# GateLoop attention and a PReLU MLP in one program: other banks for the last pair's products, and another written-out order

## The chip, the cores and the metric

The program runs on one core of a Trainium2 chip. The metric is the device time in microseconds (us) of one execution of the whole program; 787.76 us is the median of three runs before the change (786.93 to 790.6). The profile is of one further execution.

## The reference

Two stages. The first is a recurrence over 768 tokens, for 4 batches and 8 heads, with a state of 48 x 48 complex numbers per head; the second is a two-layer MLP on its output, with 384 model columns and 2048 hidden columns.

```python
mag = np.sqrt(a_re * a_re + a_im * a_im)
scale = np.minimum(mag, 0.999) / (mag + 1e-06)
a_re_n, a_im_n = (a_re * scale, a_im * scale)
...
for t in range(S):
    ar, ai = (a_re_n[:, :, t, :, None], a_im_n[:, :, t, :, None])
    new_re = ar * S_re - ai * S_im
    new_im = ar * S_im + ai * S_re
    kv = np.einsum('bhd,bhe->bhde', k[:, :, t], v[:, :, t])
    S_re, S_im = (new_re + kv, new_im)
    y[:, :, t] = np.einsum('bhd,bhde->bhe', q[:, :, t], S_re)
...
h = x @ w_in
g = np.maximum(h, 0.0) + alpha * np.minimum(h, 0.0)
return (g @ w_out).astype(np.float32)
```

The tokens of the first stage, 4 x 768 = 3072 rows of 384, are the rows `x` of the second.

## The kernel before

**Units.** The 3072 tokens are cut into 24 units of 128 tokens (six per batch). `gates` turns the inputs `a_re` and `a_im` of one or several units into phases (`phs`) and running products of decays (`decs`), on VectorE (DVE) and ScalarE (ACT), and writes them to DRAM. `loads` and `loads_v` bring `KQ` (keys and queries), `PP` (phases), `T` (decays), `V` and `VL` (values) of a unit back in. `unit` does the recurrence without a loop over tokens: for six distances (1, 2, 4, 8, 16, 32) it multiplies keys and queries by decays on DVE (L642, six times a unit), copies half of them on ACT (L665, L681), and multiplies keys by queries on TensorE (PE) into the tile `ps_lv` (L601). Then it turns the keys (L713), makes the new states from keys and values (L725, `ps_kv`; L733 and L736 on DVE), multiplies the queries by the states (L751) and the masked key-query products by the values (L765), both into `ps_y`, copies the result to the tile `T` (L778, ACT) and sends it to DRAM (L783). `loads_x` reads two units of it as `xT`, the input of the MLP for a pair of units, 256 rows.

**Weights.** The weights come as 64-bit words and are turned into 32-bit floats in sixteen pieces, by `to_f32`: three ACT steps (L439 to L443) and three DVE steps (L447, L449, L451) for each piece.

**MLP.** There are twelve pairs. `features` (L824, the first two pairs) and `two_features` (L846, the other ten) make hidden columns: products into the tile `ps_h`, which has two buffers of one PSUM bank each, then ACT (L831; L855, L859) and DVE (L833; L861). `outputs` (L874) does the second layer of the first two pairs. For the other ten `seven` does it with seven block products in place of eight (a Strassen-Winograd scheme) in half-size blocks: `product` (L960) puts 8 matmuls of 128 x 192 into the tile `ps_o`, which has one buffer, the ring that the planner calls `sums`; after each product ACT (L976) or DVE (L966, L987, L1003) adds the block to `top0` or `top1`, and L1009 and L1017 send the results to DRAM. The products of one pair are called P1, P2, T2, T1, T3, T4 and P3, in this order. Between the first two the DVE makes sums of blocks of hidden columns (L974, L982, L984, L990); T2 reads what L984 has made. A matmul of 32-bit floats stands in the trace as two matmul rows, a transpose (L713) as one: a product is 16 rows.

**Order.** All of these are Python generators. Each `yield` is a step, with a cost, the steps that it waits for and the rings that it takes a buffer of; these arguments are read by a planner that is not part of the kernel. In the kernel `step` gives `None`, `Ring.put` does nothing, and `Plan.run` takes the next step of the task that the next letter of the string `ORDER` names: A to I are the nine calls of `gates`, J `loads`, K `half_rows`, L `loads_v`, M `pieces` (raw weights), N and O `weights`, P to Z and a to m the 24 units, n `loads_x`, o `all_mlp`. The order in which letters come is the order of instructions on each engine's queue and on the queue of SP, which issues all transfers. What an instruction waits for on the chip follows from the tiles that it reads and writes. Within `all_mlp` the steps have a fixed order of their own, which `blocks`, `some` and `part` set.

```python
def step(*args, **kwargs):
    return None
DVE = ACT = POOL = PE = DMA = step
...
def run(self, order):
    for c in order:
        next(self.tasks[self.LETTERS.index(c)], None)
```

Of the kernel before, what the change touches and what calls it, by code (L numbers as in the profile page):

```python
# [31 lines left out]
    "ABMMAAAABKABBAAAAAAAAAABAAMAAAMMBNABMJKNNBAAABANNBAAAJAANABBBBBAAAAAABAAABBBBBBBJMJJAPPPMOOOOPBJJBBB"  # L32
    "BNBLBOBBBNOONNOBBBPLJJLJJJOOBBBBOBOBLMLCPPPPNNPNNPPCNPPPQPPQOPONCNPCOONOPCCJJLKKKKMLLLLLOQCCQPPPPPPP"
    "PQLLLLJJMJMJMQPPPPPQCQCQCCPQCPCPCPCPPCPPCOQCCPPQQOPPPPPPLCQCNNNCQQCLLJLJJnLJLMJLQNCOOLLJLLLLLLJMCCCC"
    "RRNOQoQCCRQCRQQQRoQQooNCCCoQoQOQooQQoNNRQCRCCQRCQCORNNoQRQQoooooOOOOQRooQQRQRQooQQooQCJQQLLLQRNORRND"
    "DLLJJSoooooooNOONORODORRORSnLLMLLLLJLLLLRDDooooRRooooooDRRoRRRSSNDooooooDoDooRooRooooMoSooSRRDDSJJJM"
    "KDoDRDoRSSSDRDDoooRoDoOooRRRRRORRSoooDDRDDoOJoooooSSLLLLLLoRDoooooDoSSoooooORRMDSoSooooSSoTDJLLLLLJJ"
    "LJLLLJKKKDDKDJSDSSoToDDDSSSTSSoooDDNDSNDNoSSoooTTSTTOSSDTODSoNToooooooNNNDOSSSSSooSSoSSSSDTTJKLNoNoo"
    "ooNoTTToTooooTLSLSDLLnLLLLLoNNTNoooNNooTTTTOTToTToJLLLLoooOoOLJToooTTOOoJEooTToUUoooooooTJJTTUUoEoTT"
    "oJJooTTUTTTUTUEoToTTUoUUooooooTLLLLLLTToVoUEoUoUUooEoUoUooooooUVLLLJVLLEUUUooUUULJJLLooJKJKJJooEUEVo"  # L40
    "oUUoooooUUVooEUUoooVoUVVUVUVVVEoooEVUUUUUUVVUoUUVEULUoVVooooooEULLLLLJJLLLJLLLJLVoEEooVooVoVVoVoooWV"
    "VVEEVVoooooooEoVoLLEoWoooooooooVEWooEoEooWoVoWWVoVEEVVVWWooooooEEJnVVVVVVLWWVoooVWVVoWVVLJWKJJLLLEJW"
    "WWWLLLLJLLELLLLEoJooooooWWooooEooWEWEEEEEoEooooXXEEXEoooWooWWWWJoooooooooooJEJooWWooWoWoooXFWWWWWXXW"
    "WXXWoooXXoooooooooooXWWWWWWWooooooooooooooooXXooooLWWLKnFJLFXXoFXFYYooooooooLLJLLLLLLLLLLJJXoooooooo"
    "oooooXXXYFXXXFooooooXXooXoooooXXoooYFFFXXooooooYYXXYXFYFYooooooYXXYoooooooooooXXXYXXXYYoXXFXXYYYoooo"
    "oooooooFoooooooYYoLLJXLJoFoooooXYFYYFFLLLJLJJLJLoYYYYooZoooooooooooZoooYooLooYoLLLLLoJJFZFooZooooooo"
    "oooooYYZZYoYZYZZZYYZFFFKJJaYooooooooooYYZFFZYYYYYYYKKLLYFFLYLLLLooooJLLnJZZoFoFooooooooFZoaZoooooooo"
    "oFooLFFFJLLLLJoooooFoooZZZZooooZFZooooaFFFFFLFoooZoooooooooooZZoooooZooooZaooooooooooJJJGZoaZaZaZZaa"
    "aoZoZoooooZZZaaoZZZaooooooooZZZZLLZZLLLLLLGGGaaaaooooooooGGooaaooaaaaoaoaaGooooooooooGGGooaooaGooaao"
    "oooooooooooobLLLLJLLaabbabJboooooooobaJJKJJJaaaabaooaaaabobbbooooooooobGbGaacLoooooobboocbooobbooooo"  # L50
    "oLJLJLLLLJLLLLJnbGcGGLJooooooooooocGooGJLLLoooobcGoooobcbbooooooobooooocGbbbbobbooobbooobbcboccGGocG"
    "bbGJdbbbbbbLoooooooooooooooGLGLLLGbbGoocoGbcooobcGcooGoooooooLbLbLooGooooocGcooooooooooooooccccccccG"
    "GodGoococoocoooooocooocoJJLLLJLLLLJJJoocddddGoocGcGoGcoooooocccccccccoJedddccododoGLccHLLLJJoooooooo"
    "oJLLLHLLLooooodddddHdeoooooHHoooooooooonLLLLLoJJoooooddoHeHHKKKdddooddoooooooooodooHoooooooooddoodod"
    "odoooeededHHdedeooHHoeeoddHoodooooooddddeeddddLdJJdLooooooooooeoeHoooeeeooooooooooooHfHooeeoefLLLLJJ"
    "LJLLLLLLLLJJJeeHeooeooooooooooeoooHHeooeoooeooHofHoooooooooooeoooefffeHefefffeeHeooHHfooooooKJHeeeef"
    "eeeoooooooeHeLLLeLLLeHLLLJJoooooooooofgffofHJLnLLLoooooooofHHoLLoHHHoooooooooHooooooffofHHoooooooogo"
    "oofffffoHHHofffoooooooogoogooooofoofooooooogfgfgffgggffoooooHJJJJohgooofffffffffgIIIhoooooooooLLffLh"
    "JJLLLLJJLLLLJJLLLooogoooggooogIgoooooooooooooooooohhhoooooogghhoooIgggIggggoIoogoooogooogogIoooooogg"
    "hhghhgooooooJooooghggghhgggggggoohhIooooIIIooooooooionhIIhJJLLLLJJLLJJLLLLoLLLLoLooooooooooooooooooI"  # L60
    "IoiooooooooiooooooooohhhhhhoIoIiiohooooooooooooooooooohohihhoioooooohhoohhihiihhhhihoIIIoIoohihhihho"
    "oooJhhiiioILLhjoooooooooooooooohooIIjiLJJLLLLLLLIIJLLIoILLLJoojooooooooiioooooooooiiIIjIiooiIIIIIIIi"
    "iioojooooioooooooooiooiiojiJJoijIioojijIijjoooooooiiiiiijiiiiiiJLnoojjjjjokJJoooooooooooLLJJLLLLLLLL"
# [36 lines left out]
def kernel(  # L100
# [422 lines left out]
    def loads_v():  # L523
        for u in range(NU):
            b, c = divmod(u, NCH)
            yield DMA(172, ("KQ", u), takes=(R["V"],))
            L = loaded[u]
            L["V"] = V = work.tile([P, HP, D2], F32, tag="V", name="V", bufs=1)
            nc.sync.dma_start(V[0:P - 16], v[b, :, 1:P - 15, c].rearrange("n p e -> p n e"))
            yield DMA(24)  # L530
            nc.sync.dma_start(V[P - 16:P - 1], v[b, :, P - 15:P, c].rearrange("n p e -> p n e"))
            if c + 1 < NCH:
                yield DMA(2)
                nc.sync.dma_start(V[P - 1:P], v[b, :, 0:1, c + 1].rearrange("n p e -> p n e"))
# [24 lines left out]
            L["Vp"] = {name: VL[:, i] for i, name in enumerate(LEVELS)}  # L559
            done["V", u] = t  # L560
# [7 lines left out]
    def unit(u):  # L568
# [149 lines left out]
        e = yield PE(0.72, e, ("V", u), *[("state", u - 1)] * (u > 0), takes=(R["misc"],) if last else (R["misc"], R["lv"]), mode=2, n=16 if last else 32)  # L718
# [223 lines left out]
    def seven(m, made):  # L942
# [20 lines left out]
        def fold(to, z, e, base, *deps, last=True):  # L963
# [3 lines left out]
            if last:  # L967
                R["sums"].put(t)
# [30 lines left out]
        yield 0  # L999
        z, e = yield from product(apart, T3, "T3", s3)  # L1000
# [4 lines left out]
        yield 0  # L1005
        z, e = yield from product(A22, T4, "T4", s4)
# [4 lines left out]
        yield 0  # L1011
        z, e = yield from product(A12, B22, "P3", s4)
# [127 lines left out]
```

## Time and profile before

| | |
|---|---|
| median of the runs | 787.76 us |
| profiled execution | 792.45 us |
| its span, first to last instruction | 790.7 us |
| what lies around the span | 1.75 us |
| instructions | 26869 |
| moved by DMA | 130.62 MB |
| granted TensorE clock, mean over the span | 0.974 |

In the views below a row of the timeline is: start, duration (both us), engine, line, operation, tiles out<-in, partitions x elements, xcount, and in brackets the engine's idle time before it and what ended it. PEld is the loading of a matmul's weights, which overlaps with PE. SPq is the queue of SP. A window row is: its length, then busy us (and instructions) of PE, PEld, DVE, ACT and POOL, the granted clock, the mean busy share of the 16 DMA engines, and GB/s. The chain of waits lists start, length and what the end of the program was waiting for at that time. Matmul ends are modelled, so lengths of matmuls are best read from start to start.

### The profile page before, as it was taken

What the parts mean: (1) busy time and instruction counts of PE and PEld (TensorE: products, weight loads), DVE (VectorE), ACT (ScalarE), POOL (GpSimd) and SP (SyncE); (2) the same over time, 40 slices, a digit from 0 to 9 for tenths busy, and PEclk for the clock granted to TensorE, in tenths of its full rate; (3) what the DMA queues carried; (4) which work ended last, traced back from release to release, by engine and by line L of the source; (5) the groups of instructions that cost most, each with busy time, mean ns of one, the idle gap of its engine ahead of it and who ended that gap; (6) DMA issues with size and microseconds to landing.
All of it is one profiled execution on the core that took longest, in us unless ns stands there. A gap on an engine that the chain in (4) does not pass through costs nothing.

```text
span 790.7 us, 26869 instructions
## 1 busy us (share of the span) xinstructions
PE 679.4 (86%) x11728; PEld 582.6 (74%) x11728; DVE 613.5 (78%) x815; ACT 493.0 (62%) x933; POOL 12.0 (2%) x48
## 2 busy tenths in 40 slices
PE   0024567698899999999999999999999999999997
PEld 0013445576676788988888888888988888989986
DVE  7899879787988899888897899786897766832331
ACT  8966978774467576777487666846768535443230
POOL 5000000000000000000000000000000000000000
PEclk9998589799999999999999999999999999999999
DMA  8998899869836865586656855683636644421000
GB/s 245 269 311 210 217 280 237 232 195 218 180 102 176 236 173 119 164 246 167 171 145 170 226 159 154 188 222 95 167 99 203 169 105 103 121 43 51 1 21 20
DMA packets 177181, 130.62 MB, mean 165 GB/s; under 512 B 66280, under 2 KB 168424, under 8 KB 176616
## 3 DMA queue, kind: packets, MB, share of 16 engines
q1 hardware_dynamic: 177064, 128.91, 61.4%
q8 instruction: 92, 1.51, 0.9%
q14 instruction: 25, 0.20, 0.1%
HBM read 100.52 MB, written 35.42 MB: 172 GB/s over the span
## 4 chain that ended last, share of the span: by engine, by line
PE 61%; DVE 11%; ACT 10%; DMA 9%; issue 4%; SPq 3%; DVEq 0%; ACTq 0%
PE ps_h L846 20%; PE ps_o L960 19%; PE ps_lv L601 4%; PE ps_o L874 4%; PE ps_h L824 4%; PE ps_y L765 4%; DVE KQ L642 4%; PE ps_kv L725 3%; DMA gate<-in_a_re_dram 2%; PE ps_y L751 2%; DMA T<-decs 2%; PE ps_kt L713 2%; DMA PP<-phs 1%; DMA decs<-gate 1%; DMA shared<-in_w_out_dram 1%
## 5 line engine op out<-in xcount | busy, mean ns | idle before, releaser
L846 PE MATMUL ps_h<-xT,w_in_sb 128*128 128x256 f32 x960 | 228.4, 383 | 1.4 <-DVE shared L861 1.1
L846 PEld LDWEIGHTS ps_h<-xT,w_in_sb 128*128 128x128 f32 x960 | 176.8, 190 | 23.3 <-DVE shared L861 1.5
L642 DVE TENSOR_TENSOR KQ<-KQ,T 96x1024 f32<-96x1024 f32 x120 | 145.9, 1217 | 39.8 <-PE ps_lv L601 21.0
L960 PE MATMUL ps_o<-w_out_sb,shared 128*128 128x192 f32 x640 | 113.8, 329 | 1.3 <-DVE top L966 0.9
L855 ACT ACTIVATE shared<-ps_h 128x512 f32<-128x512 f32 x80 | 47.7, 596 | 103.5 <-PE ps_h L846 103.4
L960 PEld LDWEIGHTS ps_o<-w_out_sb,shared 128*128 128x128 f32 x640 | 104.9, 190 | 4.6 <-DVE top L966 1.8
L861 DVE TENSOR_TENSOR shared<-shared,ps_h 128x512 f32<-128x512 f32 x80 | 54.4, 682 | 65.0 <-ACT shared L859 64.7
L960 PE MATMUL ps_o<-shared 128*128 128x192 f32 x480 | 88.1, 332 | 2.4 <-DVE top L987 1.2
L960 PEld LDWEIGHTS ps_o<-shared 128*128 128x128 f32 x480 | 77.6, 190 | 6.4 <-DVE top L987 2.8
L601 PE MATMUL ps_lv<-WQ 96*32 96x32 f32 x2304 | 35.2, 203 | 48.7 <-DVE WQ L584 29.5
L859 ACT ACTIVATE shared<-shared,al 128x256 f32<-128x256 f32 x160 | 74.6, 504 | 2.0
L601 PEld LDWEIGHTS ps_lv<-WQ 96*32 96x32 f32 x2304 | 27.0, 116 | 64.1 <-DVE WQ L584 29.5
L665 ACT COPY WQ<-KQ 96x1024 f32<-96x1024 f32 x48 | 49.9, 1040 | 37.3 <-DVE KQ L642 37.0
L824 PE MATMUL ps_h<-xT,w_in_sb 128*128 128x256 f32 (+1 forms) x240 | 55.9, 366 | 5.8 <-DMA xT<-ysc 5.3
L874 PE MATMUL ps_o<-w_out_sb,shared 128*128 128x384 f32 x128 | 55.5, 544 | 3.8 <-DVE shared L833 3.5
L824 PEld LDWEIGHTS ps_h<-xT,w_in_sb 128*128 128x128 f32 x240 | 43.6, 211 | 19.1 <-DMA xT<-ysc 5.5
L765 PE MATMUL ps_y<-A,VL 64*48 64x64 f32 x2304 | 43.2, 220 | 6.0 <-issue 6.0
L681 ACT COPY W<-KQ 96x512 f32<-96x512 f32 x48 | 30.7, 640 | 27.2 <-DVE KQ L642 25.1
L778 ACT COPY T<-ps_y 48x256 f32<-48x256 f32 x96 | 31.1, 365 | 26.4 <-PE ps_y L765 25.6
L765 PEld LDWEIGHTS ps_y<-A,VL 64*48 64x48 f32 x2304 | 36.7, 120 | 11.3 <-issue 8.9
L615 ACT ACTIVATE A<-ps_lv,columns 128x64 f32<-128x64 f32 x144 | 38.3, 330 | 10.1 <-PE ps_lv L601 10.0
L601 PE MATMUL ps_lv<-KQ,W 96*32 96x32 f32 x1536 | 23.9, 204 | 18.1 <-ACT W L681 17.9
(103 smaller groups left out, 950.9 us busy)
## 6 DMA issues: line engine op xcount, KB each, us to landing
T<-decs SPq DMA_DIRECT2D x48, 384.0 KB
PP<-phs SPq DMA_DIRECT2D x24, 387.0 KB
KQ<-in_q_dram SPq DMA_DIRECT2D x48, 192.0 KB
phs<-gate SPq DMA_DIRECT2D x14, 577.5 KB
decs<-gate SPq DMA_DIRECT2D x7, 1152.0 KB
KQ<-in_k_dram SPq DMA_DIRECT2D x40, 192.0 KB
vsc<-in_v_dram SPq DMA_DIRECT2D x24, 288.0 KB
VL<-vsc SPq DMA_DIRECT2D x48, 144.0 KB
```

Source lines behind the costliest of these rows:

```text
L601: nc.tensor.matmul(t[64 * i + j:64 * i + j + HC // 2, p], lhsT=keys(n, g), rhs=queries(n, g), start=True, stop=True)
L615: nc.scalar.activation(a[:, :, cols], t[:, :, at:at + name], AF.Copy, scale=s)
L642: nc.vector.tensor_tensor(out=x, in0=x if x0 is None else x0, in1=m, op=ALU.mult)
L665: nc.scalar.copy(z.rearrange("p i n t -> p i (n t)").rearrange("p i (m h) -> p m i h", h=h), bass.AP(tensor=KQ.tensor, offset=KQ.offset + ...
L765: nc.tensor.matmul(o, lhsT=Vp[h][64 * i:64 * i + 64, s, e_ * D:(e_ + 1) * D], rhs=a, start=False, stop=(s == 1 and h == LEVELS[-1]))
L824: nc.tensor.matmul(p, lhsT=w_in_sb[:, f // 2, kk, f % 2 * P:(f % 2 + 1) * P], rhs=x_of[m][:, kk, c * P:(c + n) * P], start=(kk == 0), stop ...
L846: nc.tensor.matmul(p[:, i], lhsT=w_in_sb[:, f // 2, kk, i * P:(i + 1) * P], rhs=x_of[m][:, kk], start=(kk == 0), stop=(kk == NK - 1))
L855: nc.scalar.activation(gt, p, AF.Relu, scale=-1.0)
L859: nc.scalar.activation(some_, some_, AF.Copy, scale=al_1[:, f + i:f + i + 1])
L861: nc.vector.tensor_tensor(out=gt, in0=gt, in1=p, op=ALU.add)
L874: nc.tensor.matmul(sums[0], lhsT=gt, rhs=w_out_sb[:, f], start=(f == start), stop=(f == stop))
L960: nc.tensor.matmul(z, lhsT=a[:, i], rhs=w[:, i], start=i == 0, stop=i == F2 - 1)
```

## The change

Four edits. `product` gets its bank from a variable `bank`: for the last pair (`m == NU // MC - 1`, that is 11) T2, T3 and P3 go to a buffer of `ps_h`, T1 and T4 stay in `ps_o`, as do P1 and P2; `fold` gives the same ring back. All other pairs keep `ps_o` for all seven. In the two other places only arguments of a step change: the state products (L725) name the step of V's last load, where they named that of VL's last load, and the copies of y (L778) no longer name the unit's state; its transfer (L783) does. And the string `ORDER` is another one, with the same number of letters of each task in all.

```diff
 ORDER = (
-    "ABMMAAAABKABBAAAAAAAAAAABAAMAAAMMBNABMJKNNBAAABANNBAAAJAANABBBBBAAAAAAABAAABBBBBBBJMJJAPPPMOOOOPBJJBBB"
...
+    "ABMAAAAAKJJBBAAAABAAAAAAABAAAAAABABAAMBBBMAKJMMAAAAAAAAAAAABJMAAAABBBBBBBNBBBBNONBJNNPPPPNJJBBBJBMJJB"
...
             nc.sync.dma_start(V[0:P - 16], v[b, :, 1:P - 15, c].rearrange("n p e -> p n e"))
-            yield DMA(24)
+            t_ = yield DMA(24)
             nc.sync.dma_start(V[P - 16:P - 1], v[b, :, P - 15:P, c].rearrange("n p e -> p n e"))
             if c + 1 < NCH:
-                yield DMA(2)
+                t_ = yield DMA(2)
                 nc.sync.dma_start(V[P - 1:P], v[b, :, 0:1, c + 1].rearrange("n p e -> p n e"))
+            done["values", u] = t_
...
-        e = yield PE(0.72, e, ("V", u), *[("state", u - 1)] * (u > 0), takes=(R["misc"],) if last else (R["misc"], R["lv"]), mode=2, n=16 if last else 32)
+        e = yield PE(0.72, e, ("values", u), *[("state", u - 1)] * (u > 0), takes=(R["misc"],) if last else (R["misc"], R["lv"]), mode=2, n=16 if last else 32)
...
-                t = yield ACT(2 * P, e, ("state", u))
+                t = yield ACT(2 * P, e)
...
-            t = yield DMA(98, ends[e_])
+            t = yield DMA(98, ends[e_], ("state", u))
...
+        bank = "sums"
+
         def product(a, w, name, after):
 
             for i in range(F2):
-                e = yield PE(0.345, after, known.get(name), takes=() if i else (R["sums"],))
-                if not i:
+                e = yield PE(0.345, after, known.get(name), takes=() if i else (R[bank],))
+                if not i and bank == "h":
+                    z = ps.tile([P, 2, MT], F32, tag="h", name="ps_h", bufs=2)[:, 0, 0:HALF]
+                elif not i:
                     z = ps.tile([P, DM], F32, tag="o", name="ps_o")[:, 0:HALF]
                 nc.tensor.matmul(z, lhsT=a[:, i], rhs=w[:, i], start=i == 0, stop=i == F2 - 1)
             return z, e
...
             if last:
-                R["sums"].put(t)
+                R[bank].put(t)
             return t
...
+        other = "h" if m == NU // MC - 1 else "sums"
+        bank = other
         z, e = yield from product(A11, T2, "T2", s2)
         t2 = yield from fold(u2, z, e, p1, t1)
         yield 0
+        bank = "sums"
         z, e = yield from product(A21, B12, "T1", s2)
...
+        bank = other
         z, e = yield from product(apart, T3, "T3", s3)
...
+        bank = "sums"
         z, e = yield from product(A22, T4, "T4", s4)
...
+        bank = other
         z, e = yield from product(A12, B22, "P3", s4)
```

In the two built programs each engine has the same number of instructions of each line. The MLP's instructions follow each other in the same order on PE, apart from the tile that three products write; what the new `ORDER` moves is where the units' and the gates' instructions and the weights' pieces stand between them, and the issue of transfers on SP's queue.

More of the change, by code (lines that the diff above doesn't have):

```diff
@@ L37 @@
[L37 to L51, printed above, removed]
@@ new lines @@
+    "LLLLLPCCLLMNNLJLLPPPQNCOCOPPPQQPPPPMMJJJPPNCOCMJOCQLCCQNRRnJLLJLLLCQOCQOLLLJJCLJCCoooQoooQORCCOQQQQC"
+    "CCNQRRQQooQQRQQRRCQQMLLLLLJMJNCNRNOOOQCNQCOCCNRooNOQQQooooRQQQRRQLLooooNQQRoooQQLQQROoooSooNRRMLLDoO"
+    "SONNNoooRLJJLLooLJLRNRMLLLLDDRROORRNRRooooRRRNRDNNOSSRSSoRRNOLJDSDoooDRSOOSSSDRoRoRRRooSRRRRDJnJJoRR"
+    "OoOLLMLRLLRMDoooSoSDoOoLJJLLLLLJJJJLLLSoSooooDDSNOSSSTSSooooSSTDooooSSSSNoooSoSOoOSDDDTSTDoSDooTTooT"
+    "SoooooooNSoDTTTDSDONDooSLMTSSooooooKSSSSSDDNJTToTSLSLLLSMnOoooTToooooJTUoLLLLLJDLLLDJLLLJoDoDJoooTTo"
@@ new lines @@
+    "oNOTTDTNTooooToTToDDooTUOToTTooDTToUDoooUNDDDTDoOoNNNDDNDoTNOooooTTUUTTTTTToTOOooOoooooooooOoTTUUoUo"
+    "UoooooooUJDJLLLLLEEToLKTVoooooVVUUUoooooooEUUUEoooooooVoKKEoUUUooLLJJEooUUEooooJLJJJLLLJoLLEooooUoVE"
+    "UUUUoUoooVUoUVVUUEEoVVUEVVoooooEEWoooEVUUUVUUVUVUUVUUooooooVoVoooooVVooVVEEVVooooWVooVEEVVooooVooooo"
+    "ooLULLLUKKEooEEoVooooELLLLLLJJLLLJJJJLLnVooJoVoVWVVVoWoooooooWWVVVVVWWWVVVVWWooWWoVEoLVVLooooooooooW"
+    "oXWEEEWWoLLLJLLJJLJJLLLLLLLJEEEWWEXoWooWWEoooooooooEEWWWWoooooWWooWWoXWXXEWoXooEEWXEXXXWEEEooooooooW"
@@ new lines @@
+    "WXWXWWWXWWXooXoWoooooLLLoXWoooooWoooooooFoXoooXXooWLLWLLJJLLLJFFXoooXXXoXXoooooooYYFFooooooooooooXoo"
+    "ooXXFooooXYFooXoooYLnJLJJLLLoooooooYYXFXooXYYYXXYooooooooFXYXXXYXYXJJZXXooooooooKKooooooYYoooooooXXX"
+    "XLLooYoFoooooooooooooooooFooLKJJJLLLLLKLKJKLJJZYZoZooooooooYZYZoYooYYYFYFYYYooooYoZZFFoYYooFoooooZZo"
+    "oooYYoYFFLLLKLLJooooooFFFYYoZFFZYYYYYYYYYoYYYZLoFFFFFaoooooooooZoaFoooooooJJLLnJLJLZoFFooZoZFooooooo"
+    "oooLooooooooFLLLLLLKLZZZFFFZoZZZoooooooZoooZFFoFFaFFoooooZoooooZoooZoZoaLLJoaZZZZZZoooaZoaaoaoaooooo"
@@ new lines @@
+    "ooooJoooooooaZZZaaZZZZoooaGZGGaaoooooJabGoooooooooooaaooaaaaooGooooooooobZZJJbJLLLLLLLLJLLJLLLLJJaGo"
+    "oGGGaaaoooooooaooooooooooGGaaoooooooooobbbGGoooooaaaGoobbaaaGGGaaaaaaGGboooooGbbabGoooooGoaLLLaLLnJo"
+    "booooooooooGoLLLLJoJLLLLLLJJJooobbbbbboooooooooooooobbbbGoGboccooooocooobbbboooobboocoobobccbcbcobco"
+    "obbcooJdooooooooobobbbbbobbboooobbbGoLKLLGGJLLLLJJLJJLJcoKLLLLLLcccGGcooooGooocGcoooooooooooocccccoc"
+    "occocoooooocooooococooococdcddddcGGGGGcoooGcGoooJGGooooccooooodddedoccccoooocoocdooooocoooooocdddLLL"
@@ L70 @@
+    "mmlmnooooooooooooooooooooooooooooooooooooooooooooooooooooooooooooooooooooooooooooooooooooooooooooooo"
     "oooooooooooooooooooooooooooooooooooooooooooooooooooooooooooooooooooooooooooooooooooooooooooooooooooo"
```

40 lines of the change are left out of this document (17 added, 23 removed).

## The prediction, made before the changed kernel was run

> **What bounds the kernel now.** I read the windows first, in three stages cut where PE's behaviour changes, then the timeline of the last one.
>
> ```profile
> 0.00:160.00 160.00, 67.46 (x1638) 53.62 (x1638) 136.14 (x201) 128.26 (x200) 10.67 (x34) 0.88 0.92 250
> 160.00:760.00 600.00, 587.62 (x9966) 507.22 (x9959) 468.87 (x601) 361.41 (x726) 1.31 (x14) 1.00 0.57 150
> 760.00:790.70 30.70, 24.34 (x133) 21.73 (x132) 8.46 (x13) 3.34 (x7) 0.00 (x0) 1.00 0.05 20
> ```
>
> In the first 160 us PE is idle for 160 - 67.46 = 92.5 us; the DMA engines are 92% busy, DVE is busy for 136 us and ACT for 128 us. PE waits there for the first units. From 160 to 760 us PE is idle for 12.4 us of 600: PE is the bound, and a step that moves there costs only what it makes PE wait. In the last stage PE has gaps again, with every other engine nearly idle:
>
> ```profile
> 764.37 2.76 PE L960 MATMUL ps_o<-w_out_sb,shared 128*128 128x192 f32 x16
> 767.55 2.87 PE L960 MATMUL ps_o<-w_out_sb,shared 128*128 128x192 f32 x16 [0.42 <-ACT top L976]
> 770.92 2.87 PE L960 MATMUL ps_o<-shared 128*128 128x192 f32 x16 [0.51 <-DVE top L987]
> 774.24 2.87 PE L960 MATMUL ps_o<-w_out_sb,shared 128*128 128x192 f32 x16 [0.45 <-DVE top L966]
> 777.56 2.87 PE L960 MATMUL ps_o<-shared 128*128 128x192 f32 x16 [0.45 <-DVE top L966]
> 781.14 2.87 PE L960 MATMUL ps_o<-shared 128*128 128x192 f32 x16 [0.71 <-DVE top L966]
> 784.46 2.87 PE L960 MATMUL ps_o<-w_out_sb,shared 128*128 128x192 f32 x16 [0.45 <-DVE top L966]
> ...
> 769.32 1.22 DVE L984 TENSOR_TENSOR shared<-shared 128x1024 f32<-128x1024 f32 x1
> 770.51 0.36 DVE L987 SCALAR_TENSOR_TENSOR top<-ps_o,top 128x192 f32<-128x192 f32 x1
> ...
> 780.74 0.35 DVE L966 SCALAR_TENSOR_TENSOR top<-ps_o,top 128x192 f32<-128x192 f32 x1
> ```
>
> These rows are P1, P2, T2, T1, T3, T4, P3. There is one `ps_o`, so each product waits until the one before it is finished and read: T2 to T1 is 774.24 - 770.92 = 3.32 us from start to start. For earlier pairs a group of L846 stands between two products and hides the reading. The chain of waits shows how long a product is then:
>
> ```profile
> 741.18 2.60 PE ps_o L960 x16
> 743.78 2.59 PE ps_h L846 x12
> ```
>
> **The tail, step by step.** With two banks the next product need not wait for the reading of the last one, so its start follows after 2.60 us.
> - P1 to P2 and P2's start stay: both are in `ps_o`.
> - T2, now in `ps_h`, no longer waits for L987, but it reads what L984 makes, and that ends at 769.32 + 1.22 = 770.54. The fold at 780.74 ends at 781.09 and T4 starts at 781.14, so a release costs 0.05 us: T2 starts at 770.59 in place of 770.92, a gain of 0.33.
> - T2 to T1: 3.32 becomes 2.60, gain 0.72. T1 needs `ps_o` free of P2, read by 770.87.
> - T1 to T3: gain 0.72. T2 is read long before.
> - T3 to T4: 781.14 - 777.56 = 3.58 becomes 2.60, gain 0.98. T3 is read by two folds (L1003 and L966), which now delay nobody: P3, next in `ps_h`, comes two products later.
> - T4 to P3: gain 0.72.
>
> Sum: 0.33 + 0.72 + 0.72 + 0.98 + 0.72 = 3.47 us; P3 starts at about 780.99. Behind P3 everything stays (one fold, one transfer). The folds that were waits are still done, 0.36 us each, under products of 2.60. If L984 were the later, only the first 0.33 would go.
>
> The page "TensorE: Matmul & The Clock Gate" of the Trainium skill, section "A second HAM failure mode: psum-queue depth-cycling", speaks against such an edit: cycling through PSUM banks can leave PE short idle gaps between groups, so that its clock falls back and forth between half and full. The trace says otherwise here: the row of the last stage above has a granted clock of 1.00, with gaps of 0.42 to 0.71 us in it. By that rule the sum would come out as in the last rival below, +9.5 in place of -3.5.
>
> **The two edits of arguments.** `step` throws its arguments away, and the built programs show no instruction added or removed on any engine. They cost and bring nothing of their own; they only let the planner write another order.
>
> **The new order.** This is the part whose size I can't read off one row. I compared the two instruction orders by what stands ahead of the same instruction on its engine, priced with these rows:
>
> ```profile
> L642 DVE TENSOR_TENSOR KQ<-KQ,T 96x1024 f32<-96x1024 f32 x120 | 145.9, 1217 | 39.8 <-PE ps_lv L601 21.0 <-ACT WQ L665 15.7 <-ACT T L778 2.7
> L302 DVE TENSOR_TENSOR_SCAN gate<-columns,gate 128x384 f32<-128x384 f32 x21 | 20.9, 1006 | 1.5 <-ACT gate L299 1.5
> L314 DVE TENSOR_TENSOR gate<-gate 128x1152 f32<-128x1152 f32 x7 | 9.5, 1353 | 0.1
> L833 DVE SCALAR_TENSOR_TENSOR shared<-shared,al,ps_h 128x128 f32<-128x128 f32 x16 | 5.3, 337 | 1.3 <-ACT shared L831 1.3
> L449 DVE TENSOR_SCALAR top<-top 128x768 uint32<-128x768 uint32 x16 | 8.7, 552 | 0.1
> L451 DVE CUSTOM_DVE_ANT_0 w_in_sb<-top,w_in_sb 128x1536 uint16<-128x1536 uint16 x8 | 7.6, 950 | 0.2
> L733 DVE TENSOR_TENSOR St<-St,T 96x384 f32<-96x384 f32 x44 | 24.1, 547 | 0.2
> ...
> 191.21 1.29 PE ps_o L874 x4
> 192.50 1.29 PE ps_h L824 x6
> ...
> 123.53 0.33 PE ps_kt L713 x4
> 125.20 0.39 PE ps_lv L601 x32
> 128.99 0.58 PE ps_y L751 x16
> 321.91 1.25 PE ps_kv L725 x64
> 437.09 1.59 PE ps_y L765 x96
> ```
>
> Units 0 to 4 come earlier. Before unit 3's last L642 DVE has three scans (3.0 us), four gate operations (L310, L312, L314, L319, 5.4 at L314's price), six L833 (2.0) and one L584 (1.2, of L642's size) less, and one L449 and one L451 (1.5) more: 10.1 us less. In return PE has less of the MLP behind it when unit 3's products end: three L874 (1.9 us), nine L824 of 256 columns (3.9) and two of 128 (0.4), 6.2 us. If DVE sets the pace, PE is 10.1 - 6.2 = 3.9 us ahead there.
>
> The weights come later, and they close the first stage:
>
> ```profile
> 175.75 1.56 PE L824 MATMUL ps_h<-xT,w_in_sb 128*128 128x256 f32 x6 [0.41 <-DVE w_in_sb L451]
> 180.44 0.91 PE L874 MATMUL ps_o<-w_out_sb,shared 128*128 128x384 f32 x2 [0.27 <-DVE w_out_sb L451]
> ```
>
> Before the last L451 DVE now has one L584, one L586 and one L642 (3.7 us), two L733 and two L736 (2.2) more, 5.9 us. PE on its side has all matmuls of one more unit behind it when it gets to the first of these: 64 rows of L601 (0.8), 8 of L713 (0.7), 64 of L725 (1.25), 32 of L751 (1.2), 96 of L765 (1.6), 5.5 us. Net 0.4 us late. At unit 5's last L642 DVE has the same work ahead in both orders but for one small instruction of L733's size. So the two ends for the first stage are -3.9 and +0.4, and the last comparison, nearest to where PE takes over, says 0. I take 0. The last raw piece of the weights stands behind some 3 MB more on SP's queue, 12 us at 250 GB/s; it was issued at 140.33 us for a conversion that ended at 180.39, so that is hidden.
>
> ```profile
> 140.33 0.39 SPq L423 DMA_DIRECT2D shared<-in_w_out_dram  x1
> ...
> 179.43 0.96 DVE L451 CUSTOM_DVE_ANT_0 w_out_sb<-top,w_out_sb 128x1536 uint16<-128x1536 uint16 x1
> ```
>
> Of the long middle stage I take 0 as well: the same instructions, PE saturated, and at most 12.4 us of idle to lose. After unit 23's last L765 two products and three groups of L846 now stand before pair 11's first group (three and three before): 5 pieces of 2.60, 13 us. Its input was issued 715.91 - 712.36 = 3.6 us after that L765 ended, and the like transfer at 506.13 took 5.0 us, 8.6 together, so it is still hidden.
>
> ```profile
> 506.13 4.96 DMA xT<-ysc
> 710.84 1.52 PE ps_y L765 x96
> ...
> 715.91 0.38 SPq L804 DMA_DIRECT2D xT<-ysc  x1
> ```
>
> **Sum.** 790.7 - 3.47 = 787.2 for the span, 792.45 - 3.47 = 789.0 for the execution with its 1.75 us around it. The profiled execution lies 4.7 us above the median, so against the runs I take the difference: 787.76 - 3.47 = 784.3 us.
>
> **Rivals.**
> *An earlier start adds to it.* Unit 3 is 3.9 us ahead and PE keeps that, because DVE, idle for 160 - 136.14 = 23.9 us of the first stage, loses less time waiting for inputs that stand 1 to 4 MB earlier on SP's queue (units 0 to 5, by the sizes of the page's transfers). 784.3 - 3.9 = 780.4; with a third of DVE's idle time instead, 8 us, 776.3. For: PE waited for the weights only 0.41 and 0.27 us in the two rows of that gate. Against: that gate is DVE work, and there is more of it ahead.
>
> *Units squeezed in the middle.* The new order sets units 18 and 20 to 23 tighter on PE: between the first and the sixth group of L601, unit 18 had 30 matmuls of L846 and 28 of L960, now 7 and 16; with the L601, L713, L725, L751 and L765 that also stand there, PE's work falls from 28 to 13 us by the prices above (0.43 for a matmul of L846, 0.325 for one of L960). In that stretch DVE and ACT must do six L642 and the copies in turn. The trace has unit 18 and the tight unit 7:
>
> ```profile
> 539.64 0.46 PE L601 MATMUL ps_lv<-WQ 96*32 96x32 f32 x30
> 568.98 0.46 PE L601 MATMUL ps_lv<-KQ 96*32 96x32 f32 x30
> ...
> 236.87 0.46 PE L601 MATMUL ps_lv<-WQ 96*32 96x32 f32 x32
> 251.08 0.49 PE L601 MATMUL ps_lv<-KQ 96*32 96x32 f32 x32
> ```
>
> 29.3 us and 14.2 us. Unit 7 shows that 14.2 can be done; two more L642-sized instructions in the way make PE wait 2.4 us for each of five units, 12 us, half of that 6. 784.3 + 6 = 790.3, at most 796. It decides from 3.5 us on, where it eats the tail's gain. For: DVE waited 21.0 and 15.7 us in L642's row for its partners in this chain. Against: DVE has 131 us free of 600 in that stage.
>
> *The tail does not overlap.* If the products still waited (one engine's read of a bank holding up writes to another), the time is 787.8. Against: L846 and L960 already alternate so at 741.
>
> *The clock falls in the tail.* PE's clock was below full where it waited often (0.88 in the first stage's row). If it went to half, the five products from T2 on would take 2.60 us more each: 13.0 - 3.5 = 9.5, and 797.3 us. Against: 1.00 in the last stage's row, with gaps of 0.42 to 0.71 before each product.
>
> **Chances and range.** The tail alone with the order within 3.5 us either way 0.45 (781 to 788); earlier start 0.18; squeezed units or a like loss in the order 0.29; no overlap 0.05; clock 0.03. The range 777 to 792 takes the first and most of the two next to it. A difference of 0.5% (3.9 us) is about what a measurement tells from no change. Faster by more means under 783.8: 0.18 and a little under half of the first case, 0.39. Slower means over 791.7: the upper part of the squeezed case, the clock, and losses of the order that I see no row for, 0.20. Within: 0.41.
>
> **What would show it.** Right: from T2 on starts 2.60 us apart with no idle time before L960, T2 within 0.1 us of L984's end; PE idle after 160 us about 12 us; the last L765 of unit 5 at the same time as before within 4 us. Wrong: gaps over 0.2 us between these products; PE waiting for L642, L665 or L681 at units 18 to 23 by more than 3.5 us in sum; a window to 160 us with PE busy by more than 5 us more or less, apart from clock.

## The result, and the profile after

| | before | after |
|---|---|---|
| median of the runs, compared on one chip | 788.14 us (4 runs) | 777.09 us (4 runs, 774.55 to 778.9) |
| ratio | | 0.9854, 95% interval 0.9817 to 0.9891 |
| profiled execution | 792.45 us | 778.9 us |
| its span | 790.7 us | 777.2 us |

The change makes the kernel 11 us faster (8.6 to 14.4 by the interval of the ratio); 3.5 us were forecast. In the kernel after, lines behind the new statements have moved by 1 to 11: L601 is L602, L642 is L643, L765 is L766, L960 is L965, L966 is L971, L984 is L989. L451 and all lines of the gates are where they were.

The windows of the kernel after, in the three stages of the prediction (length, then busy us of PE, PEld, DVE, ACT and POOL with their instructions, clock, DMA share, GB/s):

```profile
0.00:160.00 160.00, 81.10 (x1900) 64.40 (x1900) 141.73 (x209) 128.68 (x204) 11.72 (x34) 0.94 0.89 240
160.00:750.00 590.00, 580.29 (x9715) 502.27 (x9702) 463.65 (x595) 361.06 (x723) 1.31 (x14) 1.00 0.59 155
750.00:777.20 27.20, 23.18 (x133) 21.77 (x131) 8.47 (x13) 3.34 (x7) 0.00 (x0) 1.00 0.06 22
```

In the first 160 us PE is now busy for 81.1 us where it was 67.5, with 262 instructions more (1900 against 1638). The long middle stage has 9.7 us of PE idle in 590 us; it had 12.4 in 600. The timeline of the last stage of the kernel after (rows as in the timelines above):

```profile
754.28 2.76 PE L965 MATMUL ps_o<-w_out_sb,shared 128*128 128x192 f32 x16
...
757.46 2.87 PE L965 MATMUL ps_o<-w_out_sb,shared 128*128 128x192 f32 x16 [0.42 <-ACT top L981]
...
759.23 1.23 DVE L989 TENSOR_TENSOR shared<-shared 128x1024 f32<-128x1024 f32 x1
...
760.51 2.87 PE L965 MATMUL ps_h<-shared 128*128 128x192 f32 x16 [0.18 <-DVE shared L989]
...
763.22 2.76 PE L965 MATMUL ps_o<-w_out_sb,shared 128*128 128x192 f32 x16
...
765.82 2.76 PE L965 MATMUL ps_h<-shared 128*128 128x192 f32 x16
...
768.42 2.76 PE L965 MATMUL ps_o<-shared 128*128 128x192 f32 x16
...
771.02 2.76 PE L965 MATMUL ps_h<-w_out_sb,shared 128*128 128x192 f32 x16
```

T2 starts 0.05 us after L989's end (759.23 + 1.23 = 760.46), and no product behind it has idle time before it. P1 to P3 takes 771.02 - 754.28 = 16.74 us; before it took 784.46 - 764.37 = 20.09. So the banks bring 3.35 us. P1 itself starts 764.37 - 754.28 = 10.1 us earlier, and 10.1 + 3.4 is the whole difference of the spans, 13.5 us. The gain that was not forecast is made ahead of P1. Unit 4's copies of y already end at 181.3 us, 13.3 us earlier than before (194.6); unit 23's end at 706.2, 7.6 us earlier (713.8). These are two single executions, and between unit 4 and P1 the lead shrinks and grows again by some us; but it is there before 200 us and is carried through the stage in which PE is seldom short of work.

### The profile page after: what moved, and what is told of

Same layout as the page of the kernel before. It is cut to its first block, busy times and chain, and to the rows that moved or that the text cites. A ratio compares the mean times of both kernels' runs of the same rounds, so it can differ in the third digit from the quotient of the medians.

```text
span 777.2 us, 26854 instructions
## 1 busy us (share of the span) xinstructions
PE 684.6 (88%) x11728; PEld 588.4 (76%) x11728; DVE 613.9 (79%) x815; ACT 493.1 (63%) x933; POOL 13.0 (2%) x48
## 5 line engine op out<-in xcount | busy, mean ns | idle before, releaser
L847 PEld LDWEIGHTS ps_h<-xT,w_in_sb 128*128 128x128 f32 x960 | 176.6, 190 | 22.2 <-issue 0.5
L643 DVE TENSOR_TENSOR KQ<-KQ,T 96x1024 f32<-96x1024 f32 x120 | 145.8, 1216 | 25.9 <-PE ps_lv L602 13.8
L965 PE MATMUL ps_o<-w_out_sb,shared 128*128 128x192 f32 x624 | 111.9, 329 | 1.7 <-DVE top L971 0.9
L965 PEld LDWEIGHTS ps_o<-w_out_sb,shared 128*128 128x128 f32 x624 | 102.2, 190 | 5.0 <-ACT top L981 1.5
L965 PE MATMUL ps_o<-shared 128*128 128x192 f32 x448 | 81.0, 330 | 0.5 <-DVE top L971 0.5
L965 PEld LDWEIGHTS ps_o<-shared 128*128 128x128 f32 x448 | 73.0, 190 | 3.1 <-DVE top L971 0.9
L825 PE MATMUL ps_h<-xT,w_in_sb 128*128 128x256 f32 (+1 forms) x240 | 56.6, 367 | 13.3 <-DMA xT<-ysc 13.3
L602 PE MATMUL ps_lv<-WQ 96*32 96x32 f32 x2304 | 34.7, 204 | 35.1 <-DVE WQ L585 27.6
L825 PEld LDWEIGHTS ps_h<-xT,w_in_sb 128*128 128x128 f32 x240 | 44.2, 210 | 26.8 <-DMA xT<-ysc 13.4
L602 PEld LDWEIGHTS ps_lv<-WQ 96*32 96x32 f32 x2304 | 26.7, 117 | 49.7 <-DVE WQ L585 27.6
L875 PE MATMUL ps_o<-w_out_sb,shared 128*128 128x384 f32 x128 | 52.4, 518 | 3.7 <-DVE shared L834 2.8
L766 PE MATMUL ps_y<-A,VL 64*48 64x64 f32 x2304 | 48.1, 229 | 1.0 <-DMA VL<-vsc 0.9
L766 PEld LDWEIGHTS ps_y<-A,VL 64*48 64x48 f32 x2304 | 39.9, 127 | 7.5 <-issue 2.9
L602 PE MATMUL ps_lv<-KQ,W 96*32 96x32 f32 x1536 | 24.1, 204 | 15.2 <-ACT W L682 12.3
```

Of the source, the lines that this page charges most:

```text
L602: nc.tensor.matmul(t[64 * i + j:64 * i + j + HC // 2, p], lhsT=keys(n, g), rhs=queries(n, g), start=True, stop=True)
L643: nc.vector.tensor_tensor(out=x, in0=x if x0 is None else x0, in1=m, op=ALU.mult)
L766: nc.tensor.matmul(o, lhsT=Vp[h][64 * i:64 * i + 64, s, e_ * D:(e_ + 1) * D], rhs=a, start=False, stop=(s == 1 and h == LEVELS[-1]))
L825: nc.tensor.matmul(p, lhsT=w_in_sb[:, f // 2, kk, f % 2 * P:(f % 2 + 1) * P], rhs=x_of[m][:, kk, c * P:(c + n) * P], start=(kk == 0), stop ...
L847: nc.tensor.matmul(p[:, i], lhsT=w_in_sb[:, f // 2, kk, i * P:(i + 1) * P], rhs=x_of[m][:, kk], start=(kk == 0), stop=(kk == NK - 1))
L875: nc.tensor.matmul(sums[0], lhsT=gt, rhs=w_out_sb[:, f], start=(f == start), stop=(f == stop))
```

## The experiments

**Which part of the change.** Two kernels take the change apart into banks and order, two more take the order apart at the end of unit 5's steps. `rest(a, b)` stands for the letters of `a` in their sequence, without as many of each letter as `b` has.

```diff
# banks_alone: the new banks, the old order
-ORDER = NEW
+ORDER = OLD
# order_alone: the new order, all products in ps_o
-        other = "h" if m == NU // MC - 1 else "sums"
+        other = "sums"
# first_stage: as order_alone, and
-ORDER = NEW
+ORDER = NEW[:1008] + rest(OLD, NEW[:1008])
# after_that: as order_alone, and
-ORDER = NEW
+ORDER = OLD[:964] + rest(NEW, OLD[:964])
```

> The old ORDER with the changed banks of the last pair. Theory (the two halves of the change are independent, the tail is worth 3.4 us): 788.1 - 3.4 = 784.7 us, starts of T2, T1, T3, T4, P3 2.60 us apart, P1's start unchanged at 764.4 us of the span within 2. Rival (part of the tail's gain needs the new order): 786 to 788.

> The new ORDER with all seven products of the last pair in ps_o. Theory: the order is worth some 7.7 us in the medians (11.05 less the tail's 3.4) and up to 10 in the profile, so 780.4 us, gaps of 0.45 to 0.71 us back before each of the last products, P1's start near 754. Rival: 784 or more, if the order is worth no more than the forecast's range for it.

> The new ORDER up to the last step of unit 5 (its first 1008 letters), then what is left in the old ORDER's sequence; old banks. Theory (the order's gain is all made in the first 220 us): as with the whole new order, 780.4 us. Rival (half of it comes from the stalls in the middle stage): 784.

> The old ORDER up to the last step of unit 5 (its first 964 letters), then what is left in the new ORDER's sequence; old banks. Theory (gain all in the first 220 us): 788 us, as before. Rival (half of it in the middle): 784.

| | median | ratio to before (788.92 us), 95% interval |
|---|---|---|
| banks_alone | 783.29 us | 0.9934, 0.991 to 0.9958 |
| order_alone | 778.49 us | 0.9878, 0.9845 to 0.991 |
| first_stage | 779.84 us | 0.9892, 0.9846 to 0.9939 |
| after_that | 794.3 us | 1.0073, 1.0043 to 1.0102 |

The banks alone bring 3.3 to 7.1 us by the interval; in their trace P1 to P3 takes 773.80 - 757.06 = 16.74 us, the same as in the kernel after, and in order_alone 769.39 - 749.30 = 20.09, as before. The order alone brings 9.6 us by its ratio (7.1 to 12.2), and its first 1008 letters alone 8.5 (4.8 to 12.2). The rest of the new order brings nothing by itself, and this kernel is 5.8 us slower than before (3.4 to 8.0). Why it is slower its trace doesn't tell: P1 starts at 761.46 us in it, earlier than in the profiled execution of before, and its profiled execution, 789.88 us, is the second fastest of its ten runs.

The times came near what was expected for banks_alone, order_alone and first_stage; after_that was expected at 788 or 784 and missed. Two starts of P1 were missed as well: banks_alone has it at 757.06 us, 7.3 earlier than before, where the expectation had 2 at most, and order_alone at 749.30 for 754.

**Where the first stage's gain stands.** The end of the last L451 is the place at which the prediction had compared the two orders, since from there PE has all weights. Up to it PE has done 44 rows of L875 and 144 of L825 in both orders; the groups by line up to that time show 64 L602, 64 L726, 32 L752 and 96 L766 more in the new one. These are the last third of a unit's L602 and all its products behind the turned keys; its other rows stand ahead of that time in both orders. The next fences are windows up to the end of the last L451, and from there to the start of P1. First three executions with the old first stage, of before, banks_alone and after_that:

```profile
0.00:180.39 180.39, 86.98 (x1956) 67.70 (x1956) 155.08 (x234) 143.91 (x230) 10.81 (x36) 0.90 0.89 243
180.39:764.37 583.98, 572.47 (x9661) 496.97 (x9662) 450.62 (x570) 347.27 (x700) 1.17 (x12) 1.00 0.57 148
```

```profile
0.00:175.33 175.33, 84.26 (x1956) 65.08 (x1956) 154.84 (x234) 143.82 (x230) 10.84 (x36) 0.92 0.90 250
175.33:757.06 581.73, 571.53 (x9661) 496.47 (x9661) 450.13 (x570) 347.67 (x700) 1.19 (x12) 1.00 0.57 148
```

```profile
0.00:176.24 176.24, 87.03 (x1956) 67.46 (x1956) 155.07 (x234) 143.89 (x230) 10.84 (x36) 0.91 0.89 249
176.24:761.46 585.22, 572.56 (x9660) 496.68 (x9661) 451.87 (x571) 348.58 (x700) 1.18 (x12) 1.00 0.58 148
```

Then three with the new one, of the kernel after, order_alone and first_stage:

```profile
0.00:180.04 180.04, 99.51 (x2212) 78.08 (x2212) 160.16 (x241) 145.35 (x234) 11.72 (x34) 0.94 0.89 244
180.04:754.28 574.24, 566.16 (x9406) 492.35 (x9406) 445.91 (x563) 345.89 (x695) 1.31 (x14) 1.00 0.58 150
```

```profile
0.00:176.83 176.83, 96.42 (x2212) 75.04 (x2212) 160.29 (x241) 145.38 (x234) 11.25 (x34) 0.96 0.92 248
176.83:749.31 572.48, 565.39 (x9406) 491.91 (x9406) 445.99 (x563) 346.34 (x695) 1.31 (x14) 1.00 0.59 151
```

```profile
0.00:178.45 178.45, 94.60 (x2212) 73.54 (x2212) 160.02 (x241) 145.14 (x234) 11.80 (x34) 0.88 0.90 245
178.45:751.65 573.20, 565.75 (x9406) 492.16 (x9406) 444.58 (x564) 345.75 (x695) 1.32 (x14) 1.00 0.57 151
```

Means over three:

| up to P1 | old | new | difference |
|---|---|---|---|
| DVE busy before the last L451 ends | 155.0 us | 160.2 us | +5.2 |
| DVE idle before it ends | 22.3 us | 18.3 us | -4.0 |
| PE busy from there to P1 | 572.2 us | 565.8 us | -6.4 |
| PE idle from there to P1 | 11.5 us | 7.5 us | -3.9 |
| P1 starts | 761.0 us | 751.7 us | -9.2 |

The conversion comes only 1.1 us later although DVE has 5.2 us more to do before it, because DVE is idle 4.0 us less; what PE has done more by then is worth 6.4 us; and PE is idle 3.9 us less behind it. The four differences add up to -9.1, and but for rounding this is the whole gain of the order up to P1. The idle times of the two groups don't overlap: DVE's are 20.5 to 25.3 us in the old and 16.5 to 19.9 in the new order, PE's 10.2 to 12.7 and 7.1 to 8.1.

By the lists of waits up to the end of the last L451, DVE waits 2.9 us for PE in the mean of the three old executions and 0.9 in the new, 6.7 and 4.3 us for ACT, but 7.9 and 9.7 us for transfers. Behind the last L451 the whole fall of PE's idle time lies in the first 70 us, where it is 5.1 us in the old mean and 1.1 in the new. From there to P1 the stops of PE for which the profile shows no wait (below) are 5.9, 5.8 and 3.6 us in the old executions and 0.9, 1.0 and 1.2 in the new: they fell by 4.1 us in the mean, as much as the idle time. That fewer stops are why P1 comes earlier isn't shown by that; see bursts_broken.

**Single parts of the old order put back.** In three kernels the letters of the weights (M, N, O), of the gates (A to I), or of both stand, within the first 1008 letters, after as many other letters as in the order of before. Units and MLP keep their sequence, so PE's instructions stand in the order of the kernel after.

```diff
# weights_back, gates_back, gates_and_weights_back
-ORDER = NEW
+ORDER = place(NEW[:1008], like=OLD, letters="MNO" | "ABCDEFGHI" | "ABCDEFGHIMNO") + NEW[1008:]
```

> The changed kernel, in whose order the raw loads and the conversions of the weights stand again after as many other steps as in the order of before; PE's instruction order is that of the changed kernel. My theory: the gain of the first stage comes from the units' inputs and DVE work standing ahead of the weights, so that PE has unit products to do while it waited before. Then most of the gain goes: PE busy in the first 160 us falls from 81 to about 72 us, time 783 to 787 us (changed kernel 777.1). Rival: the gain lies in PE's own order of instructions (shorter runs of short matmuls, so fewer stops for which the profile shows no wait). Then the time stays at 777 to 779 us and these stops stay at about 3 us after 160 us.

> The changed kernel, in whose first stage the gates' steps stand again after as many other steps as in the order of before; PE's order is that of the changed kernel. My theory has the weights as the main cause and the gates beside them: 778 to 782 us. If the gates carry the gain: 783 to 787 us. If PE's own order carries it: 777 to 779 us.

> Both of the two edits at once: gates and weights stand again as in the order of before against the units' and the MLP's steps; what is left of the new first stage is the order of units, loads and MLP among themselves, with PE's instruction order. My theory: the gain of the first stage goes, 784 to 787 us, PE busy in the first 160 us about 70 us. Rival (PE's own order): 777 to 779 us.

Measured were 803.44, 821.32 and 807.94 us, ratios of 1.022 (1.0134 to 1.0306), 1.0462 (1.0399 to 1.0525) and 1.0311 (1.0231 to 1.0392) to a before of 786.63 us. Every expectation missed: all three are slower than either order. The windows of the first 160 us, one fence for each kernel:

```profile
0.00:160.00 160.00, 64.11 (x1527) 51.03 (x1530) 123.36 (x183) 113.80 (x182) 10.07 (x33) 0.86 0.83 228
```

```profile
0.00:160.00 160.00, 51.65 (x1373) 41.77 (x1373) 113.31 (x171) 106.36 (x163) 10.41 (x33) 0.82 0.77 208
```

```profile
0.00:160.00 160.00, 59.12 (x1445) 47.10 (x1446) 124.25 (x181) 113.76 (x172) 10.56 (x33) 0.92 0.82 224
```

DVE does 113 to 124 us of work in that time where it did 136.1 before and 141.7 after. With PE's own order kept, the time moves by 26 to 44 us, so PE's sequence alone doesn't make the gain. In the first 200 us SP's queue stands still for results of the gates (L328, L365) for 13.2 us before and 17.2 after, and for 33.7, 40.1 and 25.5 us in these three, and the transfers behind them come later; how much of the 26 to 44 us that is no run tells. That gates, conversions and transfers fit one another only as a whole is a reading. Which of them carries the gain these three don't tell.

**The two resources of the first stage, loaded one by one.**

```diff
# dve_more
-        nc.vector.tensor_tensor(out=WQ, in0=some(1, -1), in1=phases(1, 0), op=ALU.mult)
+        for _ in range(2 if u < 5 else 1):
+            nc.vector.tensor_tensor(out=WQ, in0=some(1, -1), in1=phases(1, 0), op=ALU.mult)
# queue_more
-                nc.sync.dma_start(raw, src[f])
+                for _ in range(2 if 2 <= f < 4 else 1):
+                    nc.sync.dma_start(raw, src[f])
```

> The changed kernel, with the product that makes WQ (L585, 1.14 us from start to start) done twice in units 0 to 4: 5.7 us more work on DVE before the last L451, nothing else. Theory (DVE's work sets the pace of the first stage, as the prediction counted): the last L451 and all behind it come 4 to 5.7 us later, 781 to 783 us. Rival (DVE's 18 us of idle time in that stretch take it up): under 2 us, 777 to 779 us.

> The changed kernel, with four of the sixteen raw pieces of the weights (768 KB each, number 5 to 8) loaded twice: 3 MB more on SP's queue, 12 us at 250 GB/s, nothing else. If the place on SP's queue sets the pace (the rival of the prediction): DVE waits longer for units 2 to 5, the last L451 8 to 12 us later, 785 to 789 us. If DVE's own work sets it and the transfers have slack: under 3 us, 777 to 780 us.

dve_more took 780.0 us (ratio 0.9915, 0.9882 to 0.9948, to a before of 788.31); that is 2.9 us above the median after, or 4.8 by the two ratios: between the two theories by the one, within the first by the other. Its windows:

```profile
0.00:184.57 184.57, 99.45 (x2212) 77.84 (x2212) 166.20 (x246) 145.55 (x234) 11.12 (x34) 0.84 0.89 238
184.57:762.26 577.69, 567.60 (x9405) 493.25 (x9405) 446.41 (x564) 346.46 (x695) 1.32 (x14) 1.00 0.58 149
```

DVE has 166.2 us of work and 18.4 us of idle time before the last L451 ends. The idle time is that of the three executions above (18.3), so in this execution the added work was added in full; but at 786.88 us it is the slowest of the ten. The medians say that about half of the work stays, the ratios most of it. By neither does DVE's idle time take up all of it; how much it takes up stays open.

queue_more took 792.85 us (1.0081, 1.0047 to 1.0115): 15.8 us more than the kernel after. The edit did more than add 3 MB, though. The second load of a piece writes the same tile as the first, and SP's queue waits until the first has landed: by its list of waits 21.5 us in all, at four places. Two of them (L424 is the line of these loads; each row holds both issues):

```profile
57.52 5.25 SPq L424 DMA_DIRECT2D shared<-in_w_in_dram  x2
71.75 7.45 SPq L424 DMA_DIRECT2D shared<-in_w_in_dram  x2
```

Its window of the first 160 us, and DVE's waits in the first 200 us (engine, tile and line, what it waited for: us in total, times, longest):

```profile
0.00:160.00 160.00, 63.49 (x1568) 50.67 (x1568) 126.09 (x189) 115.03 (x183) 11.16 (x33) 0.82 0.90 246
```

```profile
DVE WQ L586 <- DMA PP<-phs: 12.5, 1, 12.5
DVE gate L319 <- ACT gate L316: 7.8, 1, 7.8
```

DVE does 15.6 us less in 160 us (126.09 for 141.73), and one wait for a unit's phases is 12.5 us. So a queue that stands still for 21.5 us makes the kernel 15.8 us longer, most of it and not all. What 3 MB more would cost without these waits was not measured.

**PE's stops.** The waits of PE name "issue" where it waited for nothing that the profile shows. From 60 to 760 us, first before, then after:

```profile
PE ps_y L765 <- issue: 6.0, 4, 2.3
PE ps_lv L601 <- issue: 5.6, 3, 3.2
```

```profile
PE ps_lv L602 <- issue: 2.6, 2, 2.2
PE ps_y L752 <- issue: 0.5, 1, 0.5
```

11.6 us became 3.1. They stand at the units' short matmuls (rows of `ps_lv` and `ps_y`). Two kernels change the length of such runs.

```diff
# bursts_broken: the order of before (letters 801 to 832 and 931 to 964), with the new banks
-oJJooTTUTTTUTUEoToTTUoUUooooooTL   EoooEVUUUUUUVVUoUUVEULUoVVooooooEU
+oJJooTToooUTooTooTUTUETTTUUUooTL   EoooEVUUooUooUooUUVVUUUVEULUVVooEU
# bursts_joined: the order after, for units 8 to 15; unit 8 (X) as one of them
-XFXooXYYYXXYooooooooFXYXXXYXYX
+XFXXYYYXXYFXYXXXYXYXoooooooooo
```

> The order of before with the changed kernel's banks (measured at 783.3 us, P1 at 757.1 us), with ten steps of the MLP moved by a few places so that its long matmuls stand between L752's and L766's groups of units 4 and 5, where PE stopped 0.92 us twice without a wait that the profile shows; nothing else moves. Theory (PE runs out of instructions in long runs of short matmuls): both stops go, PE's stops of this kind after 175 us fall from 2.6 to about 0.8 us, P1 comes 1.8 us earlier against the same end of the last L451. Rival (the stops belong to a place in the instruction stream, whatever stands there): they appear somewhere else, the sum stays at 2.6 us.

> The changed kernel, with the MLP's steps that stand between the L726 and the last L766 of units 8 to 15 moved behind them, so that each of these units has its 192 to 256 short matmuls in one run, in the stage where PE is never short of work. Theory (PE runs out of instructions): stops with no wait shown, about 1 us in each of the eight units, 5 to 10 us in sum, 782 to 787 us. Rival (such stops have nothing to do with runs of short matmuls): under 1 us of such stops in 240 to 560 us; what PE loses is then named as a wait for DVE or ACT; 777 to 780 us.

bursts_broken took 788.1 us (0.9984, 0.9956 to 1.0011, to a before of 788.31). Rows of PE's timeline with such a stop between 175 and 222 us, first in banks_alone, then in bursts_broken:

```profile
183.22 0.96 PE L766 MATMUL ps_y<-A,VL 64*48 64x64 f32 x49 [0.92 <-issue]
...
190.54 0.44 PE L602 MATMUL ps_lv<-WQ 96*32 96x32 f32 x27 [0.79 <-issue]
...
210.26 0.54 PE L766 MATMUL ps_y<-A,VL 64*48 64x64 f32 x21 [0.92 <-issue]
```

```profile
187.48 0.31 PE L766 MATMUL ps_y<-A,VL 64*48 64x64 f32 x3 [0.72 <-issue]
```

By the sums of the waits from 175 to 250 us, 2.6 us of stops became 0.7, about what the theory had (0.8), but nothing is won: from the end of the last L451 to P1 it takes 583.5 us, in banks_alone 581.7, where 1.8 less were expected, and by the ratios the kernel is slower than banks_alone (0.9984 for 0.9934). In the same 75 us PE waits 3.4 us for ACT and DVE at the units' lines L602 and L714, and 0.3 us in banks_alone. So what the stops gave back turned into waits for the units' other steps.

bursts_joined took 800.22 us (1.014, 1.009 to 1.019). Waits of PE from 240 to 560 us:

```profile
PE ps_y L766 <- DMA VL<-vsc: 6.9, 4, 3.8
PE ps_y L752 <- DVE St L737: 6.4, 4, 1.9
...
PE ps_y L766 <- issue: 0.2, 1, 0.2
```

No stops of this kind arise, as the rival had it, although its time is missed by 20 us: what the MLP's matmuls had covered, the waits for the states and for V, is now bare. A run of some 200 short matmuls is not enough for a stop where PE was busy with long ones before.

**The first stage cut in half.**

```diff
# first_half: as order_alone, and (unit 2's last step is letter 511 in NEW, 578 in OLD)
+ORDER = NEW[:511] + rest(OLD, NEW[:511])
# second_half: as order_alone, and
+S = OLD[:578] + rest(NEW, OLD[:578])
+ORDER = S[:1008] + rest(OLD, S[:1008])
```

> The changed kernel's order up to the end of unit 2 only (all its steps done, about 128 us), and behind that every remaining step in the sequence of before, with the banks of before: first_stage cut in half (measured 779.8 us, against 788.9 before). If the gain is gathered evenly over the first stage, as DVE's idle time suggests (1.9 of the 4.0 us less by 110 us), the time is 783 to 786 us. If the early units alone bring it: 779 to 781 us. If it lies in units 3 to 5 (one unit's products ahead of the last conversion, PE's stops behind it): 787 to 789 us.

> The other half: the order of before up to the end of unit 2, then the changed kernel's sequence to the end of unit 5, then that of before; banks of before. If the gain is gathered evenly: 783 to 786 us. If the early units alone bring it: 787 to 789 us. If it lies in units 3 to 5: 779 to 781 us.

first_half took 787.08 us (0.9981, 0.9951 to 1.0011), second_half 788.18 us (0.9998, 0.9968 to 1.0029), to a before of 788.57. By the intervals the halves bring at most 3.9 and 2.5 us. Neither brings what both bring together (8.5 us by the ratio of first_stage), nor do their medians, 1.5 and 0.4 us, add up to it. Each of the three expectations gave at least one half a gain that neither shows. The windows of first_half, then of second_half:

```profile
0.00:176.64 176.64, 93.78 (x1956) 72.08 (x1956) 155.13 (x234) 143.45 (x230) 11.36 (x36) 0.93 0.89 249
176.64:756.82 580.18, 572.08 (x9660) 497.40 (x9661) 449.96 (x570) 347.38 (x700) 1.18 (x12) 1.00 0.56 149
```

```profile
0.00:190.08 190.08, 96.82 (x2212) 76.84 (x2212) 160.70 (x241) 145.78 (x234) 10.80 (x34) 0.94 0.84 231
190.08:764.05 573.97, 567.04 (x9406) 493.35 (x9405) 444.59 (x564) 345.45 (x695) 1.31 (x14) 1.00 0.57 150
```

The second half does move the extra products ahead of the last L451 (2212 instructions), and the time from there to P1 is the short one, 574.0 us. But its last L451 ends at 190.1 us, some 13 us later than in the old order's mean, with 29.4 us of DVE idle (190.08 - 160.70) instead of 22.3. The first half leaves the work by then as it was (1956) and its end, too, at 176.6. Only with both are the extra products done and the conversion in time. The reading is that the gain needs the early units' new places for the late ones to fit in. It rests on one trace of each half, and that of the second is 792.11 us, 3.9 above its median.

## Why the prediction was right or wrong

**The tail was right.** 3.47 us were forecast, 3.35 measured, with the starts that it named: T2 0.05 us behind L989's end, then 2.71, 2.60, 2.60 and 2.60 us apart. Its rivals fell: no product waits for the reading of another, and the granted clock of the last stage is 1.00. What the Trainium skill tells of a bf16 kernel that cycles through PSUM banks (page "TensorE: Matmul & The Clock Gate", section "A second HAM failure mode: psum-queue depth-cycling"), a clock that swings between half and full, does not show here: the products alternate between banks, and the clock stays full.

**The new order failed, at "I take 0".** The step compared what stands ahead of the last L451 on DVE (5.9 us more) with what PE has behind it when it gets there (5.5 us), net 0.4 late. Both sizes were near: DVE has 5.2 us more work, PE's work is 6.4 us (the 8 rows of L713 in the 5.5 stand ahead in both orders). What it left out is that idle time doesn't stay the same when an order changes. DVE is idle 4.0 us less before that point and PE 3.9 us less behind it, together 7.9 of the 9.2 us. The bounds, -3.9 and +0.4, were made from the same count and shared the omission. The rival that named this gave 780.4 and, for more of DVE's idle time, 776.3 us; 777.09 came out. That this still lies inside the range, by 0.1 us, is luck: no row gave the third of DVE's idle time. A chance of 0.18 for it was too low for a stage in which DVE is idle 23.9 us of 160.

**The rival's reason is not borne out.** It held that DVE loses less time waiting for inputs that stand earlier on SP's queue. queue_more shows that a queue that stands still is costly. But DVE's waits for transfers didn't fall, neither up to the last L451 (7.9 and 9.7 us in the means) nor in the first 240 us of before and after (8.6 and 11.4). Those for PE and ACT fell. Rows of the lists up to the end of the last L451, first before, then after:

```profile
DVE gate L275 <- DMA gate<-in_a_re_dram: 5.2, 4, 2.3
DVE KQ L642 <- PE ps_lv L601: 3.9, 5, 1.5
DVE KQ L642 <- ACT WQ L665: 2.9, 2, 1.8
```

```profile
DVE gate L275 <- DMA gate<-in_a_re_dram: 5.2, 4, 2.3
DVE WQ L585 <- DMA PP<-phs: 3.9, 1, 3.9
...
DVE KQ L643 <- PE ps_lv L602: 1.6, 2, 1.2
...
DVE KQ L643 <- ACT WQ L666: 1.3, 2, 0.8
```

3.9 us in five waits of a unit's next L642 for PE's L601 became 1.6 in two (1.5 and 3.2 in banks_alone and after_that, 0.3 and 0.8 in order_alone and first_stage). It fits the reading that in the new order other work of DVE stands between a unit's steps while PE and ACT answer, but no run takes these waits alone, so why DVE is idle less stays open.

**Unit 3's lead** was put at 3.9 us, and at unit 5's last L642 the two orders were called equal. Unit 3's copies of y end 11.3 us earlier, unit 5's last L642 9.6 (193.9 for 203.5). These are differences of two single executions, which say little below some 5 us (last section).

**The middle stage was right at 0.** From 545 to 720 us, where units 18 to 23 stand, the waits of PE show none on the units' lines, against the 3.5 us that would have spoken for squeezed units; the longest wait on such a line after 240 us is 1.4 us, at 302 us. What PE lost less behind the first stage it lost less before some 250 us. The edits of arguments add no instruction, and no run takes them apart from the order that was written with them.

**The sign that the prediction named for being wrong** was the right one to look at: the window to 160 us, with PE busy by more than 5 us more. It is 13.6.

## What to carry to other kernels

Where no engine is full, counting the work ahead of a step on its engine gives the length of the queue but not the time: the idle time between is as large as the effect, it changes with the order, and the bounds have to take it in (here 17 to 25 us of DVE's 180). Compare two orders at the point where the bound passes to one engine, by two numbers: when the last step that it needs ends, and how much of that engine's work is done by then. And don't expect half of a reordering to bring half of its gain: here neither half's gain could be told from zero.

## What the hardware showed that was not expected

**PE's stops end where its instructions arrive.** 92 packets of 16384 bytes go over the queue that the profile calls "instruction" in each execution, which is one for every 255 of PE's 23,456 rows. All 66 of PE's stops of over 0.35 us between 50 and 760 us for which the profile shows no wait, in the fifteen traces of this study, end 2.2 to 3.1 us after the start of such a packet; the packets are 7.9 us apart in the mean, so chance would put about one stop in nine there. That PE waits for such a packet is inferred from this; no run changes the supply. Some of the stops:

```
            PE goes on at   stop      since the packet's start
before       71.5 us      1.68 us    2.33 us
before      139.9 us      3.15 us    2.91 us
before      217.2 us      2.31 us    2.56 us
after       130.5 us      2.23 us    2.71 us
```

The Trainium skill, page "Runtime: NRT & Kernel Launch", section "Instruction fetch mechanics", has the blocks of 16 KiB and 256 instructions, and says that crossing such a boundary is mostly hidden. By this reading it is not always in this kernel: 11.6 us of stops before, 3.1 us after, the longest 3.2 us. By bursts_broken a shorter run of short matmuls removes a stop, and by bursts_joined a run of 200 after long matmuls doesn't make one; how much of a lead PE's supply has was not measured.

**One and the same start varies by 5 us.** The programs of before, banks_alone, after_that and bursts_broken have the same instructions up to the last L451. Their last L451 ends at 180.4, 175.3, 176.2 and 179.2 us. Before and banks_alone are the same even up to P1, and it starts at 764.37 and 757.06 us. A difference of two single traces says little below that size; the means of three above are what the reading rests on.
